# Linear attention with a GLU on one core: w_phi read by heads and spread by small products, weights queued behind the last row transpose

## The chip, the cores and the metric

The kernel runs on one core of a Trainium2 chip. The metric is the device time of one execution in microseconds (us). A core has five engines that run side by side, each with its own instructions in a fixed order: TensorE (PE, matmuls into PSUM), VectorE (DVE), ScalarE (ACT), GpSimd (POOL) and SyncE (SP), which here issues all DMAs. Engines wait for each other through semaphores. An instruction that waits holds up everything behind it on its engine.

## The reference

The input x has 2048 rows of 640. There are 32 heads of 20, and the FFN is 1536 wide.

```python
def _A_ref(x, wqkv, w_phi, wo):              # H = 32, Dh = 20
    q, k, v = ...                            # x @ wqkv, split by heads
    pq = einsum("bhsd,hdf->bhsf", q, w_phi)  # w_phi: [32, 20, 20]
    pk = einsum("bhsd,hdf->bhsf", k, w_phi)
    phi_q = concatenate([softmax(pq), softmax(-pq)], -1)
    phi_k = concatenate([softmax(pk), softmax(-pk)], -1)
    kv = einsum("bhsf,bhsd->bhfd", phi_k, v)
    z = phi_k summed over s
    o = einsum(phi_q, kv) / (einsum(phi_q, z) + 1e-6)
    return o.reshape(B, S, D) @ wo
h = x + _A_ref(layernorm(x), wqkv, w_phi, wo)
return h + ((layernorm(h) @ w_gate) * (layernorm(h) @ w_up)) @ w_down
```

## The kernel before

All matmul inputs are bf16. The rows are 16 tiles of 128 (t = 0 to 15); 640 columns are five chunks of 128.

`build_graph` lists 975 operations, each with an engine, an estimated cost, what it reads and writes, and a key. `schedule` plays the list with the estimated costs and, on each engine, always takes the ready operation with the smallest key. That fixes the order on every engine, the semaphore waits and the PSUM banks. The keys come from a table, `TUNED`, which names each operation with a planned start time (and, after a colon, the other engine where an operation can run on either). So a changed table changes the order of all engines.

The stages, with the names that the prediction uses:

- **Head.** `zero` and `warm` give TensorE matmuls on zeros. SP loads x (`x0`, `x1`, `x2`, ...; from `x2` on two tiles in one DMA), the K columns of Wqkv (`wk0`, `wk2`, `wk4`) and the V columns (`wv0`, ...). w_phi is read twice: `phr`, its first 600 rows of 20 values, one row in each descriptor, onto 120 partitions, and `ph5`, the last 40 rows. GpSimd builds an identity matrix (`id0`, `id1`) and a mask `GL` of which row belongs to which head (`gl0`, `gla`, `glb`), and multiplies them into the block-diagonal matrix `Phi` (`phi0`, `phi5`). TensorE transposes Wk (`WT0` to `WT4`), the transposes are copied out (`WTe`), and the folds `F1_0` to `F1_4` multiply them by Phi, so that K's projection gives pk at once (`Fe1` copies out). The same for Wq: `wqt0` to `wqt5` are DMA transposes from DRAM, and `F0_0` to `F0_4` fold; each needs all six.
- **Rows.** For each tile VectorE takes the statistics (`L1s`, `L1a`), ScalarE the inverse deviation (`L1l`, `L1e`, for groups of tiles), VectorE normalizes (`xn`). Tiles 0 to 2 are transposed by TensorE (`xt`, `xte`), the others by a DMA transpose on SP (`xt3` to `xt15`). Then come the projections `V` (copied out by `Ve`) and `K`, two exponentials on ScalarE (`Kx`), the sums and their reciprocals on VectorE (`Ks`, `Kr`), the scaling on GpSimd (`Kn`), and `KV`, which adds the tile's part to three PSUM banks. A projection holds a pair of banks until it is copied out. V and K of tiles 0 and 1 are split into five parts each (`V0_0`, ...).
- **Columns and output.** Q's projections (`Q`, `Qx`), the attention output by tile (`N`, `sr`, `rho`, `A`, `B`, `dd`, `rd`, `o`, a DMA transpose `oT`, the product with Wo `O`, the sum `h`), the second normalization (`L2s`, ..., `hc`, a DMA transpose `hT`), the gate and up products (`U`, `g`, `u`) and the down product (`D`, `y`, a store `w`).

`PACE` holds loads back until a named row transpose has been issued on SP:

```python
for g in range(6):
    PACE[7 + g // 2].append(wqt(g, 10 * (7 + g // 2) - 19))
PACE[10] += [wrows("wo", ..., 0, 2, 328, 81), wrows("wo", ..., 2, 5, 492, 81)]
for c in range(NC):
    PACE[11 + c] += [wrows("wg", ...), wrows("wu", ...)]
```

The lines of the profile that matter: L268 all plain loads, L299 the Wq transposes, L331 `phi0`, L357 the warming matmuls, L367 Wk's transposes on TensorE, L388 the folds, L404, L405 and L407 the row statistics, L432 `xn`, L440 the row transposes on TensorE, L448 the row transposes on SP, L461 the K and V projections, L482 the exponentials, L485 and L488 `Ks` and `Kr`, L490 `Kn`, L499 `KV`, L233 copies, L520 Q, L553 the attention products, L596 the product with Wo, L600 the sum `h`, L635 gate and up, L654 down.

Of the kernel before, what the change touches and what calls it, by code (L numbers as in the profile page):

```python
# [12 lines left out]
P = 128  # L13
# [22 lines left out]
WIN = [0, 120, 240, 360, 480, 512]  # L36
# [6 lines left out]
NWARM = 8  # L43
# [5 lines left out]
x0:1.18 wk0:2.14 wk2:3.58 wk4:3.1 x1:0.7 wv0:5.02 wv2:5.98 wv4:5.5 x2:4.06 x4:6.46 x6:4.54 phr:1.66 ph50:2.02 ph5:2.62 x8:14.747 x10:23.167 x12:25.347  # L49
x14:23.647 wqt0:24.127 wqt1:25.827 wqt2:35.727 wqt3:39.867 wqt4:41.087 wqt5:38.647 wo0:36.947 wo2:43.527 wg0:32.327 wu0:32.807 wg1:50.547 wu1:46.927  # L50
wg2:49.587 wu2:44.007 wg3:48.627 wu3:51.027 wg4:50.067 wu4:49.107 id0:0.7 gl0:2.62 eps:1.82 id1:2.22 gla0:3.68 glb0:4.34 gla4:4.12 glb4:4.56 gla1:3.24
glb1:4.78 gla2:3.02 glb2:5.72 gla3:3.46 glb3:3.9 phi0:5 phi5:5.94 va1:1 glx:6.191 kv1:6.591 zero:0.7 warm:1.08 WT0:5.718 WTe0:6.323 WT1:6.053
WTe1:6.781 WT2:8.355 WTe2:9.249 WT3:8.69 WTe3:9.979:1 WT4:6.509 WTe4:7.114 F1_0:7.402 Fe1_0:7.974:1 F1_1:7.704 Fe1_1:8.276:1 F1_2:10.189 Fe1_2:10.761:1
F1_3:10.919 Fe1_3:11.491 F1_4:8.054 Fe1_4:8.625:1 L1s0:4.081 L1a0:5.081 L1s1:3.261 L1a1:4.901 L1s2:9.027 L1a2:11.597 L1s3:9.847 L1a3:11.487 L1s4:14.167
L1a4:15.517 L1s5:13.347 L1a5:14.987 L1s6:11.817 L1a6:12.817 L1s7:10.667 L1a7:11.707 L1s8:21.717 L1a8:22.997 L1s9:19.367 L1a9:21.607 L1s10:25.947
L1a10:27.227 L1s11:27.337 L1a11:28.977 L1s12:31.767 L1a12:34.007 L1s13:28.157 L1a13:39.087 L1s14:35.857 L1a14:37.097 L1s15:34.577 L1a15:39.197
L1l0:5.411 L1e0:5.841 L1l1:5.191 L1e1:5.631 L1l2:12.114 L1e2:12.544 L1l4:15.846 L1e4:17.312 L1l8:29.338 L1e8:30.181 L1l12:39.614 L1e12:40.044 xn0:6.361
xt0:7.123 xte0:7.811:1 xn1:5.941 xt1:6.844 xte1:7.393:1 xn2:15.097 xt2:15.941 xte2:16.689 xn3:12.927 xt3:13.527 xn4:18.527 xt4:20.727 xn5:18.107
xt5:19.507 xn6:18.947 xt6:21.947 xn7:17.687 xt7:18.287 xn8:30.927 xt8:34.507 xn9:36.677 xt9:37.427 xn10:31.347 xt10:33.287 xn11:30.507 xt11:31.107
xn12:44.327 xt12:45.707 xn13:41.187 xt13:42.307 xn14:43.907 xt14:47.407 xn15:43.487 xt15:44.487 V0_0:11.594 V0_1:13.767 V0_2:14.311 V0_3:14.854  # L60
# [159 lines left out]
def build_graph():  # L220
# [61 lines left out]
    for n_, (a, b_) in enumerate(((0, 2), (2, 4), (4, 5))):  # L282
# [7 lines left out]
        lambda: T["A_wphi"].rearrange("h d f -> (h d) f")[0:600, :].rearrange("(g p) f -> p g f", p=120), 24, [phr_b], key=-98.5)  # L290
    G.op("pool", "ph50", lambda e: e.memset(T["ph5"][:, :], 0.0), 0.2, LP, [], [ph5_b], -99.2)
    dma("sp", "ph5", lambda: T["ph5"][88:128, :], lambda: T["A_wphi"].rearrange("h d f -> (h d) f")[600:640, :], 2, [ph5_b],
        reads=[ph5_b], key=-98.4)


    PACE = {t: [] for t in range(NT)}
# [718 lines left out]
```

## Time and profile before

| what | value |
|---|---|
| median of 8 runs | 286.04 us (284.24 to 287.48) |
| the profiled execution's own time | 287.46 us |
| its span, first to last instruction | 285.7 us |
| TensorE busy | 277.6 us (97%) |
| VectorE busy | 182.7 us (64%) |
| ScalarE busy | 106.1 us (37%) |
| GpSimd busy | 56.7 us (20%) |
| share of the chain that ended last | PE 81%, DVE 9%, DMA 6% |
| DMA | 44832 packets, 22.31 MB |

All times in the profile count from the first instruction. The windows give, for a stretch of time, each engine's busy time and the number of its instructions, the granted TensorE clock, the busy share of the DMA engines and GB/s. The waits give who waited for whom. The chain in order of time is followed back from the last instruction, and gives start, length and what it was. In a timeline line, the brackets at the end give the idle time ahead of the group and what ended it.

### The profile page before, as it was taken

To read this page: it belongs to the slowest core of one execution; us is meant where nothing else is said; L and a number is where in the kernel's file an instruction comes from. 1 tells how busy PE (TensorE), PEld (TensorE's weight loads), DVE (VectorE), ACT (ScalarE), POOL (GpSimd) and SP (SyncE) were. 2 spreads that over 40 slices of the span, in tenths; PEclk is the share of its full clock that TensorE was granted. 3 is DMA by queue.
4 is the path that set the end of the run, shared out by engine and by line. 5 is a ranking of instruction groups with operands and counts; after the bars stand their busy time and mean duration, and the time that the engine had idled before them with its cause. 6 is when DMAs were issued, how large, how long until landed. Compare 5 with 4: busy or idle time off the path is not lost.

```text
span 285.7 us, 5039 instructions
## 1 busy us (share of the span) xinstructions
PE 277.6 (97%) x2083; PEld 184.2 (64%) x2083; DVE 182.7 (64%) x370; ACT 106.1 (37%) x187; POOL 56.7 (20%) x64
## 2 busy tenths in 40 slices
PE   6999889999999999999999999999999999999996
PEld 3877657779555589775555544576565555478875
DVE  4799899677258787997798562635982144332533
ACT  3786645643786852224131323110221022312110
POOL 7023369978011121222000000001000000000000
PEclk9999999999999999999999999999999999999999
DMA  6737499990002368134310320021115000100002
GB/s 165 251 78 172 100 203 154 251 328 12 0 2 46 61 127 237 39 86 78 69 37 13 68 46 2 0 70 48 47 28 66 23 25 24 23 2 23 25 23 69
DMA packets 44832, 22.31 MB, mean 78 GB/s; under 512 B 35977, under 2 KB 43529, under 8 KB 44809
## 3 DMA queue, kind: packets, MB, share of 16 engines
q1 hardware_dynamic: 44809, 21.99, 33.3%
q8 instruction: 16, 0.26, 0.4%
q14 instruction: 7, 0.06, 0.1%
HBM read 11.00 MB, written 2.62 MB: 48 GB/s over the span
## 4 chain that ended last, share of the span: by engine, by line
PE 81%; DVE 9%; DMA 6%; SPq 2%; issue 1%; ACT 0%; DVEq 0%
PE ps L635 36%; PE ps L654 18%; PE ps L596 8%; PE ps L520 8%; PE ps L553 4%; PE ps L461 3%; DMA xnT<-xn 3%; DVE SR L485 3%; DVE xn L432 2%; PE ps L499 2%; DMA x_all<-in_A_x_dram 1%; DVE st L405 1%; DMA scratch<-in_A_wqkv_dram 1%; DVE st L404 1%; SPq L268 1%; DVE SR L488 1%
## 5 line engine op out<-in xcount | busy, mean ns | idle before, releaser
L635 PE MATMUL ps<-xnT,Wgu 128*128 128x512 bf16 (+1 forms) x600 | 108.1, 337 | 0.0
L635 PEld LDWEIGHTS ps<-xnT,Wgu 128*128 128x128 bf16 x600 | 58.2, 98 | 42.2 <-DVE ev L643 0.4
L640 ACT ACTIVATE scratch<-ps 128x512 bf16<-128x512 f32 (+1 forms) x60 | 30.6, 511 | 106.7 <-PE ps L635 102.7
L643 DVE TENSOR_TENSOR ev<-ps,scratch 128x512 bf16<-128x512 f32 (+1 forms) x60 | 33.5, 578 | 35.2 <-ACT scratch L640 19.5
L654 PE MATMUL ps<-Wp,ev 128*128 128x320 bf16 (+2 forms) x396 | 54.1, 295 | 0.0
L461 PE MATMUL ps<-Wp,xnT 128*128 128x320 bf16 x320 | 45.9, 300 | 2.8 <-DMA xnT<-xn 1.5
L654 PEld LDWEIGHTS ps<-Wp,ev 128*128 128x128 bf16 x396 | 38.0, 98 | 14.3
L490 POOL TENSOR_TENSOR ev<-ev,SR 128x1280 bf16<-128x1280 bf16 x16 | 37.3, 2356 | 26.4 <-DVE SR L488 20.6
L461 PEld LDWEIGHTS ps<-Wp,xnT 128*128 128x128 bf16 x320 | 30.6, 98 | 14.8 <-DMA xnT<-xn 2.0
L666 DVE SCALAR_TENSOR_TENSOR Wp<-ps,rs,x_all 128x640 bf16<-128x640 f32 (+3 forms) x18 | 14.6, 810 | 31.6 <-PE ps L654 31.6
L610 POOL TENSOR_SCALAR ln<-mv 128x1 f32<-128x1 f32 x16 | 3.9, 243 | 115.7 <-DVE mv L609 112.1
L482 ACT ACTIVATE ev<-ps 128x640 bf16<-128x640 f32 x32 | 20.8, 701 | 10.9 <-PE ps L461 10.0
L485 DVE TENSOR_REDUCE SR<-ev 128x64 f32<-128x1280 bf16 x16 | 23.0, 1455 | 2.5 <-ACT ev L482 2.5
L529 ACT ACTIVATE eqT<-ps 128x512 bf16<-128x512 f32 x40 | 21.6, 596 | 7.4 <-PE ps L520 7.4
L596 PE MATMUL ps<-Wo,scratch 128*128 128x320 bf16 x160 | 24.0, 300 | 0.0
L520 PE MATMUL ps<-xnT,Wp 128*128 128x512 bf16 x100 | 23.0, 379 | 0.0
L615 ACT ACTIVATE xn<-x_all,mv 128x640 bf16<-128x640 bf16 x16 | 13.1, 826 | 22.6 <-DVE mv L609 19.4
L596 PEld LDWEIGHTS ps<-Wo,scratch 128*128 128x128 bf16 x160 | 15.6, 98 | 7.5
L585 POOL TENSOR_TENSOR scratch<-scratch,sm 128x640 bf16<-128x640 f32 x8 | 10.2, 1270 | 44.8 <-DVE sm L582 42.2
L600 DVE TENSOR_TENSOR x_all<-ps,x_all 128x640 bf16<-128x640 f32 x16 | 13.1, 818 | 5.5 <-PE ps L596 5.4
L520 PEld LDWEIGHTS ps<-xnT,Wp 128*128 128x128 bf16 x100 | 9.5, 98 | 9.8 <-DVE KVm L506 0.2
L553 PE MATMUL ps<-KVm,eqT 128*128 128x154 bf16 (+1 forms) x192 | 15.5, 222 | 0.0
(56 smaller groups left out, 204.9 us busy)
## 6 DMA issues: line engine op xcount, KB each, us to landing
out_dram<-Wp SPq DMA_DIRECT2D x15, 160.0 KB, 1.8
x_all<-in_A_x_dram SPq DMA_DIRECT2D x7, 320.0 KB, 4.3
Wgu<-in_B_w_gate_dram SPq DMA_DIRECT2D x5, 384.0 KB, 6.7
Wgu<-in_B_w_up_dram SPq DMA_DIRECT2D x5, 384.0 KB, 4.7
Wp<-in_B_w_down_dram SPq DMA_DIRECT2D x4, 480.0 KB, 5.1
scratch<-in_A_wqkv_dram SPq DMA_DIRECT2D x2, 320.0 KB, 4.1
Wp<-in_A_wqkv_dram SPq DMA_DIRECT2D x2, 320.0 KB, 6.2
Wo<-in_A_wo_dram SPq DMA_DIRECT2D x1, 480.0 KB, 4.8
```

What stands on the lines that cost most here:

```text
L461: ins = e.matmul(pb(b, hb)[:, 0:320], lhsT=T["xnT"][:, NC - 1 - c, P * t:P * (t + 1)], rhs=T["Wp"][:, kind, c, 320 * hb:320 * (hb + 1)], s ...
L482: G.op("act", "Kx%d_%d" % (t, s), lambda e, s=s, b=b, ek=ek: e.activation(out=T["ek"][:, ek.slots[0], s, :].rearrange("p (b n) -> p b n", ...
L485: G.op("dve", "Ks%d" % t, lambda e, ek=ek, sr=sr: e.tensor_reduce(out=T["SR"][:, sr.slots[0], 0, :], in_=T["ek"][:, ek.slots[0], :, :].rea ...
L490: G.op("pool", "Kn%d" % t, lambda e, ek=ek, sr=sr: e.tensor_tensor(out=T["ek"][:, ek.slots[0], :, :].rearrange("p s (h f) -> p (s h) f", f ...
L520: ins = e.matmul(pb(b)[:, 0:n], lhsT=T["Wp"][:, 0, i, P * c:P * (c + 1)], rhs=T["xnT"][:, NC - 1 - i, o0:o0 + n], start=(i == 0), stop=(i ...
L529: G.op("act", "Qx%d_%d_%d" % (q, c, s), lambda e, s=s, c=c, o0=o0, n=n, b=b: e.activation(out=T["eqT"][:, s, c, o0:o0 + n], in_=pb(b)[:, 0 ...
L553: ins = e.matmul(pb(b, y)[:, 22 * h0:22 * (h0 + j1 - j0)], lhsT=T["eqT"][:, s, c, P * t:P * (t + 1)], rhs=T["KVm"][:, OFF[s, c] + j0:OFF[s ...
L596: ins = e.matmul(pb(b, hb)[:, 0:320], lhsT=T["oT"][:, oT.slots[0], c, :], rhs=T["Wo"][:, c, 320 * hb:320 * (hb + 1)], start=(c == 0), stop ...
L635: ins = e.matmul(pb(b)[:, 0:n], lhsT=T["Wgu"][:, gu, c, P * ft:P * (ft + 1)], rhs=T["xnT"][:, NC - 1 - c, o0:o0 + n], start=(c == 0), stop ...
L640: G.op("act", "g%d_%d" % (bi, ft), lambda e, pg=pg, gt=gt, n=n: e.activation(out=T["gt"][:, gt.slots[0], 0:n], in_=pb(pg)[:, 0:n], func=AF ...
L643: o_ = G.op("dve", "u%d_%d" % (bi, ft), lambda e, pu=pu, gt=gt, hh=hh, ft=ft, n=n: e.tensor_tensor(out=T["hh"][:, hh.slots[0], ft, 0:n], i ...
L654: ins = e.matmul(pb(b, hb)[:, 0:w], lhsT=T["hh"][:, hh.slots[0], ft, P * tt:P * (tt + 1)], rhs=T["Wd"][:, ft, c0 + w * hb:c0 + w * (hb + 1 ...
```

## The change

- `w_phi` is read once (`w32`), with one head on each of 32 partitions (400 values in one row), as the first DMA of SP. `phr`, `ph5`, the memset `ph50` and GpSimd's `phi0` and `phi5` are gone.
- `PH`: 20 matmuls with the identity as the moving operand turn it to 20 partitions; `PHd` copies that out and reorders it; `PS`: two matmuls with a selection matrix `sel` repeat it on 120 partitions; `PHe` on VectorE multiplies it by the mask `GM` into `Phi`. GpSimd makes `sel` and `GM` by three copies.
- The last window of the Wk and Wq transposes starts at 520 instead of 512, and the folds take 120 rows from it.
- The warming matmuls are 6 instead of 8, in three pairs that have a place in the order (`warm0`, `warm1`, `warm2`).
- Wo's and the FFN's weights are held back until `xt15` has been issued.
- Three estimates of the planner are changed, and the whole table `TUNED` is new: nearly all engines have another order.

```diff
-WIN = [0, 120, 240, 360, 480, 512]
+WIN = [0, 120, 240, 360, 480, 520]
-NWARM = 8
+NWARM = 6
...
-    dma("sp", "phr", lambda: T["phr"][0:120, :, :],
-        lambda: T["A_wphi"].rearrange("h d f -> (h d) f")[0:600, :].rearrange("(g p) f -> p g f", p=120), 24, [phr_b], key=-98.5)
...
+    dma("sp", "w32", lambda: T["w32"][:, :], lambda: T["A_wphi"].rearrange("h d f -> h (d f)"), 30, [w32_b], key=-100.5)
...
-    PACE[10] += [wrows("wo", lambda: T["Wo"], "A_wo", wo_b[0:2], 0, 2, 328, 81), wrows("wo", lambda: T["Wo"], "A_wo", wo_b[2:5], 2, 5, 492, 81)]
+    PACE[15] += [wrows("wo", lambda: T["Wo"], "A_wo", wo_b[0:2], 0, 2, 328, 81), wrows("wo", lambda: T["Wo"], "A_wo", wo_b[2:5], 2, 5, 492, 81)]
     for c in range(NC):
-        PACE[11 + c] += [wrows("wg", lambda: T["Wgu"][:, 0], "B_wg", [wg_b[c]], c, c + 1, 393, 91 + 10 * c),
+        PACE[15] += [wrows("wg", lambda: T["Wgu"][:, 0], "B_wg", [wg_b[c]], c, c + 1, 393, 91 + 10 * c),
...
-    G.op("pool", "phi0", lambda e: e.tensor_tensor(
...
-    G.op("pool", "phi5", lambda e: e.tensor_tensor(
...
-        for _ in range(NWARM):
+        for _ in range(2):
...
-    G.op("pe", "warm", warm, 0.43 * NWARM, LT, [z_b], [wm_b], -200)
+    for k in range(NWARM // 2):
+        G.op("pe", "warm%d" % k, warm, 0.86, LT, [z_b], [wm_b], -90)
...
+    def rows(e):
+        for f in range(DH):
+            ins = e.matmul(pb(pq_b, f // 10)[0:DH, H * (f % 10):H * (f % 10 + 1)],
+                           lhsT=T["w32"][:, :].rearrange("h (d f) -> h f d", f=DH)[:, f, :], rhs=T["ident"][0:H, 0:H],
+                           start=(f % 10 == 0), stop=True, skip_group_check=True)
+        return ins
+    G.op("pe", "PH", rows, 1.2, LT, [w32_b, id_b], [pq_b], -95)
...
+    evac("PHd", phd, 640, [pq_b], [pd_b], -95)
...
+    def spread(e):
+        for k in range(2):
+            ins = e.matmul(pb(pr_b, k)[0:120, 0:320], lhsT=T["sel"][0:DH, :], rhs=T["phid"][0:DH, 320 * k:320 * (k + 1)],
+                           start=True, stop=True)
+        return ins
+    G.op("pe", "PS", spread, mm_c(320, 320), LT, [sel_b, pd_b], [pr_b], -95)
...
+    G.op("dve", "PHe", mask, 0.8, LD, [pr_b, gm_b], [phi_b], -95)
...
-                    K = P if g == 5 else 120
+                    K = 120
...
-        G.op("dve", "xn%d" % t, xn, 0.42, LD, [x_b[t], mv_b[t], rs_b[t]], [xb], 10 * t - 22)
+        G.op("dve", "xn%d" % t, xn, 0.5, LD, [x_b[t], mv_b[t], rs_b[t]], [xb], 10 * t - 22)
...
-                bw += o.dma / (210.0 if bw < 7.0 else 370.0)
+                bw += o.dma / (210.0 if bw < 4.0 else 370.0)
...
-                bw = max(bw, now + 1.85) + 0.5
+                bw = max(bw, now + 1.7) + 0.65
```

The orders that follow from the new table, as far as the prediction uses them:

```
PE before  warm WT0 WT1 WT4 xt1 xt0 F1_0 F1_1 F1_4 WT2 WT3 K0_0 K1_0 K0_1 K1_1 F1_2 F1_3 V0_0 K0_2 K1_2 V1_0 ...
           ... K5 V6 KV1 K7 KV2 V11 K11 V10 KV3 V8 K8 K9 KV4 V9 KV5 F0_1 KV6 K13 K10 KV7 K12 KV8 V14 ...
PE after   warm0 warm1 PH warm2 PS WT1 WT0 WT2 WT3 F1_1 F1_0 xt0 WT4 xt1 F1_2 V0_0 V1_0 ... V1_3 V0_4 F1_3 K0_0 ...
           ... KV0 K6 KV1 V6 K7 V8 KV2 V10 K10 KV3 K11 V11 KV4 F0_3 KV5 V9 K8 KV6 K9 K12 KV7 V13 K13 V14 KV8 K14 K15 KV9 ...
SP before  x1 x0 phr wk0 ph5 wk4 wk2 x2 x6 wv0 wv4 wv2 x4 xt3 x8 xt7 xt5 xt4 xt6 x10 x14 wqt0 x12 wqt1 xt11 wg0 wu0
           xt10 xt8 wqt2 wo0 xt9 wqt5 wqt3 wqt4 xt13 wo2 wu2 xt15 xt12 wu1 xt14 wg3 wu4 wg2 wg4 wg1 wu3 oT1 ...
SP after   w32 x0 x1 wk0 wk2 x2 wk4 wv0 x6 wv2 wv4 x4 xt3 x8 xt4 xt5 x10 xt7 wqt1 wqt0 x12 xt6 x14 xt8 wqt3 xt10 xt11
           wqt2 xt9 wqt4 wqt5 xt12 xt13 xt14 xt15 wu1 wg2 wg3 wo2 wg0 wu0 wg1 wg4 wo0 wu3 wu4 wu2 oT0 ...
DVE after  ... L1s9 Ks0 L1a9 Ks2 L1s11 L1s10 Kr0 Ks1 L1a10 L1a11 Kr1 L1s12 L1s14 xn8 Ks4 xn10 xn11 Kr2 Ks3 L1s13 Kr3 xn9
           Ks5 Kr4 Kr5 Ks6 L1a12 L1a14 L1s15 Kr6 Ks7 L1a15 L1a13 Kr7 Ks11 xn12 Kr11 xn13 xn14 Ks10 xn15 ...
```

## The prediction

> **What bounds the kernel now.** I read the page first, then the windows, the waits of TensorE, the chain in order of time, and the timeline of the first 15 us.
>
> ```profile
> span 285.7 us, 5039 instructions
> ...
> PE 277.6 (97%) x2083; PEld 184.2 (64%) x2083; DVE 182.7 (64%) x370; ACT 106.1 (37%) x187; POOL 56.7 (20%) x64
> ...
> PE 81%; DVE 9%; DMA 6%; SPq 2%; issue 1%; ACT 0%; DVEq 0%
> ```
>
> TensorE is busy for all but 8.1 us. A change can only gain where those 8.1 us lie, or where TensorE works slowly. The windows (stretch, its length, busy time of PE first) say where.
>
> ```profile
> 30.00:35.00 5.00, 3.98 (x37) 2.85 (x36) 3.87 (x8) 2.90 (x7) 2.23 (x1) 1.00 0.41 105
> ...
> 40.00:45.00 5.00, 3.67 (x34) 2.62 (x33) 4.93 (x10) 2.45 (x6) 5.00 (x3) 1.00 1.17 168
> ...
> 50.00:55.00 5.00, 4.59 (x54) 3.64 (x52) 2.74 (x4) 2.76 (x5) 4.92 (x4) 1.00 0.95 251
> 55.00:58.20 3.20, 3.01 (x38) 2.40 (x36) 2.92 (x3) 2.40 (x5) 2.07 (x1) 1.00 1.06 248
> ...
> 70.00:283.20 213.20, 213.20 (x1478) 135.42 (x1475) 124.69 (x265) 64.79 (x117) 15.13 (x25) 1.00 0.21 46
> ```
>
> From 58.2 to 283.2 us PE never idles, so whatever the change does later counts only if it tears a hole there. Between 30 and 58.2 us PE loses 1.02 + 1.33 + 0.41 + 0.19 = 2.95 us, and 0.42 us more between 10 and 15. The rest lies before 5.94 us and after 283.2 us. The waits of PE from 12 to 60 us and the chain name the causes:
>
> ```profile
> PE ps L461 <- DMA xnT<-xn: 1.5, 2, 1.3
> PE ps L461 <- ACT ev L482: 1.0, 1, 1.0
> PE ps L388 <- ACT ev L233: 0.4, 1, 0.4
> ```
>
> ```profile
> 2.23 3.67 DMA scratch<-in_A_wqkv_dram
> ...
> 27.54 4.16 DMA x_all<-in_A_x_dram
> ...
> 36.98 4.97 DMA xnT<-xn
> ...
> 53.93 4.21 DMA xnT<-xn
> ```
>
> A row transpose that meets no other traffic lands 2.6 us after its issue (the least of the 13 of this stage); those issued behind Wo and FFN weights took 4.2 to 5.0. The first cost PE 1.33 us (V10 waits for xt10), the other 0.19. The 1.02 us at 32.5 starts at x12: it lands at 31.70, 4.16 us after issue, VectorE sits on its L1s13 with L1a11 behind it, so ScalarE's L1l8 and the exponentials behind that come late, and the PSUM pair for V6 with them. The 0.41 us is F0_1, which also needs the last Wq transpose: wqt4 landed at 50.98.
>
> In the head, the timeline:
>
> ```profile
> 1.24 3.60 PE L357 MATMUL ps<-zero 128*128 128x512 bf16 x8 [1.24 <-DVE zero L352]
> ...
> 5.94 2.10 PE L367 MATMUL ps<-ident,scratch 128*128 128x128 bf16 x18 [1.10 <-DMA scratch<-in_A_wqkv_dram]
> ...
> 5.12 1.19 POOL L331 TENSOR_TENSOR Phi<-phr,GL 120x600 bf16<-120x600 bf16 x1 [1.30 <-DMA phr<-in_A_w_phi_dram]
> ...
> 10.54 0.83 PE L367 MATMUL ps<-ident,scratch 128*128 128x128 bf16 x12
> ```
>
> 18 transposes take 2.10 us at 5.94 (0.107 apart), 12 of the same shape 0.83 at 10.54 (0.056 apart): the clock came up at about 10.5 us, after 4.6 us without a gap. The 3.60 us of warming matmuls, followed by 1.1 us of idleness, did not bring it. 4.6 us at half pace cost 2.3 us of PE time.
>
> **The change part by part.** *w_phi's read.* phr is 600 rows of 40 bytes, issued ahead of wk0. It takes 3.3 us for 23 KB, and while its small packets run (3.0 to 4.3 us) the queues move some 50 KB/us against 340 to 400 beside them. wk0, 320 KB, therefore takes 3.67 us where x0 and x1 took 2.3. Now w_phi is 32 rows of 800 bytes ahead of everything, and ph5 is gone too. That gives about 1.2 us back to every load behind it: wk0 lands at about 4.6 instead of 5.89, x2 at 6.6 to 7.5 instead of 9.31.
>
> *Phi's new path.* All of it is extra work on three in-order engines. PE: warm0, warm1 (4 x 0.43 from 1.24, to 2.95), then PH, 20 matmuls of 32 columns. The nearest rows are the folds, 21 in 1.79 us at the slow clock (0.085 each, wider pieces), and KV, 12 in 0.68 (0.057): 1.15 to 1.7 us, I take 1.4, to 4.35. w32 stands first in SP's queue and lands by 3.1 (x1, 160 KB, did), so PH hardly waits. ScalarE's PHd is like its other 640-element evacuations, 0.70, to 5.25. Then PS, two 320-column matmuls at the slow clock, 0.55, to 5.85. VectorE's PHe is like L600 (640 elements out of PSUM, 0.82), to 6.85. Queued behind PS on PE stands WT1, behind PHe on VectorE WTe1, xn0 and the rows. So WT1 starts at about 5.85 although its data is there at 4.6: against 5.94, almost nothing of wk0's 1.3 us reaches PE. Phi is ready 0.2 us later than before (phi5 ended at 6.67), ahead of the first fold (8.90 before). Price both ways: if PH takes 1.7 us and w32 is 0.5 late, PE starts 0.7 later than before; if PH takes 1.15, 0.3 earlier.
>
> *GpSimd.* It loses phi0 (1.19), phi5 (0.25) and a memset (0.40); it gains three copies, by the copies of GL (0.21) and KVm (0.50) 0.6 to 1.0 us together. va1 (1.23) moves behind them. All of it ends before 8 us; the first Kn stood at 19.45, so this is nothing. WIN's last window and K = 120 change no column count: nothing.
>
> *The clock.* Two fewer warming matmuls, but they are spread so that PE is occupied from 1.24 us on, with PH and PS between them, into the transposes. By the row (4.6 us of gapless work from 5.94 before it rises) it would come at about 10.3 and gain 0.1 us of PE. If the pieces before WT1 count as occupation, it comes 4.6 us after 1.24, about 6, and 4 us of work run at full pace: 2 us of PE time. It cannot all be used. ScalarE has PHd, WTe0, WTe2, Fe1_1, Fe1_0, xte1, Fe1_2, WTe4, WTe3 in a row (0.7 to 0.81 each), and F1_3 waits for WTe3. I followed this: F1_3 ends at 13.3 with the early clock, at 14.6 with the late one. Before, the same amount of PE work (nine parts of V, four folds) was done at 14.8. So the head gives 1.5 to 0.2 us; I take 1.05, because the pieces are close together.
>
> The Trainium skill (TensorE: Matmul & The Clock Gate, Part 1) says that the clock rises after one busy window of about 3.4 us, whose phase is free, and (Part 4) that transposes do not count as busy. The second half speaks against the change, since PH and PS are short and transposes follow; the trace has three of its 4.6 us before the rise in transposes. By Part 1 the rise falls between 4.7 and 8.1 us, a head gain of about 1.5; by Part 4 it would wait for the folds, and the gain is 0.2 or nothing.
>
> *Weights behind xt15.* Twelve loads (4.6 MB) leave the stretch from 36 to 58 us. The row transposes xt8 to xt15 then meet only the Wq transposes. For V10 I expect the landing in 2.7 to 3.5 us, not 4.97, so 1.33 and 0.19 go. The weights start at about 53 us; the last six of before landed 0.97 us apart, so twelve are in by about 68. Wo's first reader stood at 89.7 us in the chain, the FFN's at 101.7; some 3 us sooner each, that is 18 us of cover. Past it, each us would cost one. SP has nothing to do between them and the first oT.
>
> *What is late next.* The Wq transposes and x loads are reordered. x14 is issued behind wqt1, wqt0, x12 and xt6, at about 26, and lands 3.2 to 4.3 us later (x10 and x12 before): VectorE's L1s14, with xn8, Ks4, Kr2 behind it, can stall 0.3 to 1.3 us; Kn2 (2.36) follows Kr2, and KV2 waits on PE 0.1 to 1.1 us: 0.5. F0_3 waits for wqt5, issued at about 40.5 behind xt9, which waits for VectorE's xn9; the Wq transposes landed after 3.5 to 5.0 us, so at 44 to 45.5, and PE is there at about 44.6: 0 to 0.9, I take 0.3. K12 needs xn12, with one Ks more ahead of it than before, but VectorE starts its rows some 2 us sooner (x2). Sum of the waits 0.8 instead of 2.95, with bounds of 0.1 and 3.3: a gain of 2.15 (2.85 to a loss of 0.35).
>
> **Sum.** The profiled execution took 287.46 us, 285.7 of span and 1.76 around it; it stands 1.42 above the median of 286.04, and no view says where. 287.46 - 1.05 - 2.15 = 284.3. Best ends: 287.46 - 1.5 - 2.85 = 283.1; worst ends: 287.46 - 0.2 + 0.35 = 287.6. As the median may lie lower than the profiled run for a cause that both kernels share, I let the range begin 1.2 below the best end.
>
> **The rivals.** First: the head gives nothing. The clock rises no sooner and VectorE, which carries the chain from 10.21 to 52.75 almost without a break, sets the pace. Head 0.2, waits 1.3: 285.6, within 0.5% of the median. For it: VectorE is full from 10 to 25 and from 35 to 50 us, and PHe is added to it. Against: its idle 1.8 us between 25 and 35 came from late loads. That w_phi's packets were not what slowed wk0 belongs here too.
>
> Second, slower: F0_3 on PE behind wqt5. Everything on PE stands behind F0_3, and wqt5 stands behind xn9 on VectorE and xt9, wqt4 on SP. If x14 stalls VectorE for 1.3 us more and wqt5 needs 5.0 us, F0_3 waits about 3.4 us: 284.3 + 3.4 = 287.7. From a landing of wqt5 after 48 us it decides. For it: before, the same kind of fold waited, and PE arrives sooner now. Against: no weights stand in the queue, and four row transposes in a row landed in 2.6 to 2.7 us each.
>
> Third, weights late for O0: from 87 us on; with 18 us of cover, 0.01.
>
> **How the numbers follow.** Forecast with its better ends 0.64, the first rival 0.20, the second 0.15, the third 0.01. About 0.5% (1.43 us) is what a measurement of this kernel can tell from no change: faster is below 284.6, slower above 287.5. So faster 0.64, same 0.20, slower 0.16. The range reaches from 281.9 to 287.2, into the second rival; its own for the forecast is 281.9 to 284.6.
>
> **What would show it.** Right: wk0 landed before 5 us and WT1 waiting for PS; transposes 0.056 apart before 8 us; xt10 to xt15 landing within 3.5 us; PE's idle time between 30 and 58 us near 1 us and none after. Wrong: transposes at 0.107 until 10 us (head), a wait of PE at F0 for scratch or at KV for ev above 1 us, or any idle PE after 60 us, which the sum does not hold.

## The result, and the profile after

The changed kernel takes 288.58 us in the median (287.45 to 289.32, 12 runs); the kernel before took 286.24 beside it (33 runs). The ratio is 1.0076, with a 95% interval of 1.0054 to 1.0098: slower by about 2.2 us, where 284.3 had been forecast, and outside the range.

The page of the changed kernel shows the same span and the same busy time of TensorE as before:

```profile
span 285.7 us, 5087 instructions
...
PE 277.6 (97%) x2103; PEld 183.9 (64%) x2103; DVE 180.5 (63%) x366; ACT 109.3 (38%) x190; POOL 59.5 (21%) x67
...
PE 85%; DVE 7%; DMA 4%; issue 1%; POOL 1%; ACT 0%; SPq 0%; DVEq 0%
```

The two profiled executions, 287.46 and 287.45 us, are a poor pair: the one of before is near the top of its runs (284.24 to 287.57), the one after is the lowest of its twelve. What that is worth is taken up below.

The windows, with the length and PE's busy time first, answer to those of before in the prediction. One stretch of before that is not among them comes first:

```profile
10.00:30.00 20.00, 19.58 (x168) 14.54 (x166) 19.04 (x42) 16.05 (x28) 4.84 (x3) 1.00 0.55 138
```

and after the change:

```profile
10.00:30.00 20.00, 18.65 (x173) 13.86 (x171) 18.50 (x44) 16.07 (x29) 2.12 (x1) 1.00 0.69 133
30.00:35.00 5.00, 5.00 (x49) 3.86 (x48) 2.58 (x6) 3.06 (x8) 2.56 (x2) 1.00 0.31 74
...
40.00:45.00 5.00, 4.93 (x51) 3.94 (x52) 5.00 (x10) 2.39 (x4) 4.77 (x4) 1.00 0.72 131
...
70.00:283.20 213.20, 212.93 (x1470) 134.91 (x1468) 123.37 (x262) 64.03 (x117) 19.38 (x28) 1.00 0.20 46
```

The holes at 30 to 35 and 40 to 45 us are closed, as forecast. A larger one stands between 10 and 30 (1.35 us idle instead of 0.42), and a small one after 70. The waits of TensorE from 12 to 135 us name them:

```profile
PE ps L488 <- DMA xnT<-xn: 1.3, 1, 1.3
PE ps L526 <- POOL ev L517: 0.4, 1, 0.4
PE ps L623 <- DMA scratch<-scratch: 0.3, 1, 0.3
PE ps L415 <- ACT ev L232: 0.2, 1, 0.2
```

The first is V7 waiting for the row transpose xt7, which landed 4.50 us after its issue; the second KV2 for Kn2; the third O for the transpose of o; the fourth F0_3, for a copy of ScalarE's. The head is in the timeline:

```profile
1.24 1.89 PE L341 MATMUL ps<-zero 128*128 128x512 bf16 x4 [1.24 <-DVE zero L336]
...
3.06 0.93 PE L359 MATMUL ps<-ident,w 32*20 32x32 bf16 x20
...
3.92 1.03 PE L341 MATMUL ps<-zero 128*128 128x512 bf16 x2
4.02 2.97 ACT L232 ACTIVATE phid<-ps 20x640 bf16<-20x640 f32 x1 [1.95 <-PE ps L359]
...
7.13 0.75 PE L374 MATMUL ps<-phid,sel 20*120 20x320 bf16 x2 [2.18 <-ACT ln L439]
...
7.82 2.74 PE L394 MATMUL ps<-ident,scratch 128*128 128x128 bf16 x24
```

PHd takes 2.97 us and ends at 6.99. PS waits for it (the bracket names the short `ln`, which stands behind PHd on ScalarE and ended last), and PE stands still for 2.18 us. WT1 starts at 7.82, where the first transpose of before started at 5.94, and still runs at half pace (24 transposes in 2.74 us).

**Where the time lies.** To compare kernels whose orders differ, I worked out from each trace a lag: the time t, less the useful TensorE work begun by t (transposes, folds, projections, KV; not warming, PH or PS), every matmul at its price with the clock up (0.056 us for 128 columns, 0.136 for 320). It is all that the kernel has lost so far. The last two columns are the profiled execution's time and where the granted clock came up (from the trace's record; for e17, which has none, from the spacing of its transposes). The windows above give the clock as 1.00 even in the head, where the transposes run at half pace: its record has no entry ahead of the first rise. So the clock of the head is read from that rise and from the spacing of the matmuls.

| kernel | lag at 16 us | at 32 | at 44 | at 60 | its time | clock up |
|---|---|---|---|---|---|---|
| before | 8.76 | 8.78 | 11.66 | 12.76 | 287.46 | 10.54 |
| before, once more (b2) | 6.75 | 8.10 | 9.08 | 10.53 | 285.17 | 5.42 |
| after | 9.46 | 10.91 | 11.79 | 12.33 | 287.45 | 10.69 |
| e1 | 7.69 | 9.05 | 10.30 | 11.54 | 287.01 | 8.74 |
| e2 | 8.76 | 8.78 | 10.30 | 10.59 | 285.23 | 10.37 |
| e4 | 7.13 | 8.37 | 10.17 | 12.22 | 286.86 | 5.92 |
| e5 | 6.99 | 8.37 | 8.95 | 9.40 | 283.98 | 5.63 |
| e10 | 8.35 | 9.79 | 10.98 | 12.01 | 286.86 | 7.00 |
| e16 | 7.53 | 7.73 | 8.69 | 10.45 | 285.41 | 5.45 |
| e17 | 6.99 | 7.28 | 7.86 | 8.18 | 282.78 | 6.69 |

Time less the lag at 60 us is 274.6 to 274.7 for every kernel with the old path, and 274.9 to 275.5 with the new one, whose PE waits 0.3 to 0.7 us once more at about 130 us. So the lag at 60 us accounts for nearly the whole difference between these executions. Against the profiled execution of before, the changed kernel loses 0.70 in the head (9.46 against 8.76), gains 1.13 between 16 and 60 us (2.87 against 4.00), and gives 0.42 back later.

### The profile page after: what moved, and what is told of

It is laid out like the page before. It is cut to its first block, busy times and chain, and to the rows that moved or that the text cites. A ratio compares the mean times of both kernels' runs of the same rounds, so it can differ in the third digit from the quotient of the medians.

```text
span 285.7 us, 5087 instructions
## 1 busy us (share of the span) xinstructions
PE 277.6 (97%) x2103; PEld 183.9 (64%) x2103; DVE 180.5 (63%) x366; ACT 109.3 (38%) x190; POOL 59.5 (21%) x67
## 4 chain that ended last, share of the span: by engine, by line
PE 85%; DVE 7%; DMA 4%; issue 1%; POOL 1%; ACT 0%; SPq 0%; DVEq 0%
PE ps L662 36%; PE ps L681 17%; PE ps L547 8%; PE ps L488 7%; PE ps L623 7%; PE ps L580 4%; PE ps L526 3%; DMA x_all<-in_A_x_dram 3%; DVE SR L512 1%; DMA scratch<-scratch 1%; DVE st L431 1%; DVE st L432 1%; DVE xn L459 1%; PE ps L394 1%; POOL ev L517 1%
## 5 line engine op out<-in xcount | busy, mean ns | idle before, releaser
L612 POOL TENSOR_TENSOR scratch<-scratch,sm 128x640 bf16<-128x640 f32 x11 | 14.0, 1270 | 77.9 <-DVE sm L609 76.9
L580 PEld LDWEIGHTS ps<-KVm,eqT 128*128 128x128 bf16 x192 | 12.9, 98 | 4.2
```

Source lines behind the costliest of these rows:

```text
L580: ins = e.matmul(pb(b, y)[:, 22 * h0:22 * (h0 + j1 - j0)], lhsT=T["eqT"][:, s, c, P * t:P * (t + 1)], rhs=T["KVm"][:, OFF[s, c] + j0:OFF[s ...
```

## The experiments

Each was timed beside the kernel before, whose median was 285.9 to 286.2 in all of them; ratios are to that, with their 95% intervals.

### The parts one by one: e1 to e4

**e1**, the changed kernel with PHd written contiguously:

```diff
-        return copy(e, eng, T["phid"][0:DH, :].rearrange("p (h b f) -> p b f h", b=2, f=10),
-                    T["PS3"][0:DH, k:k + 2, 0:320].rearrange("p b (f h) -> p b f h", h=H))
+        return copy(e, eng, T["phid"][0:DH, :].rearrange("p (b n) -> p b n", b=2), T["PS3"][0:DH, k:k + 2, 0:320])
...
-            in0=T["PS3"][0:120, k:k + 2, 0:320].rearrange("p b (h f) -> p b h f", f=DH),
...
+            in0=T["PS3"][0:120, k:k + 2, 0:320].rearrange("p b (f h) -> p b h f", h=H),
...
```

(PHe's output and its mask are reordered with it.)

> The changed kernel with PHd writing its 640 elements in PSUM order, contiguously; the reordering by head moves into PHe's read of PSUM. Nothing else differs, nor does any engine's order. Theory H (the strided write of PHd, 2.97 us, is what holds PE 2.18 us in front of PS and delays the first fold to 10.35): PHd takes 0.7 to 0.8 us, PS starts at about 5.0, PHe takes 0.8 to 1.0, WT1 starts when wk0 lands, about 6.2 instead of 7.82, F1 at about 8.8, and the median comes 1.3 to 2.3 us under the changed kernel's 288.6: 286.3 to 287.3. Rival R (the time goes into the new order of the body, not into the head): PHd gets as fast, but the time stays at 288.0 or more. Second rival (PHe's strided read of PSUM takes over what PHd loses): PHe rises above 2 us.

Measured: 287.06 us, ratio 1.0031 (1.0012 to 1.0051), 1.5 us under the changed kernel. Its timeline:

```profile
4.03 0.69 ACT L232 ACTIVATE phid<-ps 20x640 bf16<-20x640 f32 x1 [1.96 <-PE ps L359]
...
5.71 0.82 DVE L380 TENSOR_TENSOR Phi<-ps,GM 120x640 bf16<-120x640 f32 x1 [0.24 <-PE ps L373]
...
6.04 2.74 PE L393 MATMUL ps<-ident,scratch 128*128 128x128 bf16 x24 [0.36 <-DMA scratch<-in_A_wqkv_dram]
```

The strided write alone made PHd 2.97 instead of 0.69 us. PHe, which now hops 128 bytes from element to element in PSUM, still takes 0.82. Theory H holds, and WT1 waits for wk0 at 6.04. But the kernel stays slower than before, and 24 transposes still take 2.74 us.

**e2**, the kernel before with the weights alone held back, behind the row transpose that is last in its own order:

```diff
-    PACE[10] += [wrows("wo", ...), wrows("wo", ...)]
+    PACE[14] += [wrows("wo", ...), wrows("wo", ...)]
-        PACE[11 + c] += [wrows("wg", ...), wrows("wu", ...)]
+        PACE[14] += [wrows("wg", ...), wrows("wu", ...)]
```

> The kernel before with one edit: Wo and the FFN weights wait behind the transpose that ends its own order of rows (xt14), nothing done to w_phi. Theory W (the second part of the change is a gain by itself): xt8 to xt15 land in 2.6 to 3.0 us as in the changed kernel, TensorE's idle time between 30 and 60 us falls from 2.95 to 1.2 to 1.6, the median is 284.5 to 285.2. Rival (VectorE sets the pace there, and the waits come back elsewhere): 285.9 to 286.5. Second rival (the weights arrive late): a wait of PE on a weight load after 80 us, over 286.5.

Measured: 284.49 us, ratio 0.995 (0.9927 to 0.9973). xt11, xt10, xt8, xt9, xt15, xt12 and xt14 landed in 2.6 to 3.0 us, xt13, behind wqt4, in 3.5. The waits of PE from 12 to 135 us are:

```profile
PE ps L461 <- ACT ev L482: 1.3, 1, 1.3
PE ps L461 <- ACT Wp L233: 0.3, 1, 0.3
```

Theory W holds: in the old order this half of the change is a gain of about 1.5 us (1.7 by the medians, 1.4 by the ratio), and no weight is late.

**e3**, the kernel before with the new path for w_phi (strided PHd) alone. Seen from the changed kernel, these go back to what they were, and the table and the planner's estimates with them:

```diff
-NWARM = 6
+NWARM = 8
...
-    PACE[15] += [wrows("wo", ...), wrows("wo", ...)]
+    PACE[10] += [wrows("wo", ...), wrows("wo", ...)]
-        PACE[15] += [wrows("wg", ...), wrows("wu", ...)]
+        PACE[11 + c] += [wrows("wg", ...), wrows("wu", ...)]
...
-    for k in range(NWARM // 2):
-        G.op("pe", "warm%d" % k, warm, 0.86, LT, [z_b], [wm_b], -90)
+    G.op("pe", "warm", warm, 0.43 * NWARM, LT, [z_b], [wm_b], -200)
```

> The kernel before with the first part of the change alone: w_phi read with one head per partition and spread by small matmuls, PHd with its strided write; the table of times, the eight warming matmuls in one piece and the places of the weights stay those of the kernel before. Theory H: PHd takes about 3 us, the folds' Phi is ready at 8.5 to 9, F1_0 starts 0.5 to 1.5 us later than in the kernel before, median 287.0 to 288.5. Rival (the head's time is hidden behind the load of x and of wkn): 286.0 to 286.5.

Measured: 290.86 us, ratio 1.0188 (1.0151 to 1.0225), worse than either theory said. PHd (2.94 us) stands behind L1l on ScalarE; PE waits 1.43 us for it ahead of PS and 0.57 for wk0. The record of the clock has a step that I had not expected: up at 5.63 us, down again at 9.05, up at 12.46, each 3.413 us from the last.

**e4**, the kernel before with 11 warming matmuls instead of 8, so that PE is occupied until WT0:

```diff
-        for _ in range(NWARM):
+        for _ in range(11):
```

> The kernel before with 11 warming matmuls instead of 8, so that PE is occupied from 1.24 us to where WT1 starts, about 5.9; nothing else differs. Theory C (the rise of the granted clock follows from unbroken occupation of PE, and its place in the head is worth about a microsecond): the WT transposes run 0.056 us apart from before 8.1 us on, the median is 284.8 to 285.5. Rival (the rise comes at about 10.5 whatever PE does before): 286.0 to 286.5.

Measured: 285.79 us, ratio 1.000 (0.9979 to 1.0022). The clock was up at 5.92 and the lag at 16 us 1.63 lower than in the profiled execution of before, as theory C says; by 60 us only 0.54 of it was left. With the weights still among the transposes, PE waited 1.74, 0.65, 1.05 and 0.48 us between 30 and 58 us. In this execution the gain in the head was given back in the stage behind it, and the median shows none either.

### The clock, and the order: e5 to e12

**e5**: the edits of e2 and e4 together.

> The weights held behind xt14 as in e2, and 11 warming matmuls instead of 8. In e4 the longer warming brought the clock up at 5.92 and an earlier head, but waits for row transposes after 30 us took that back; with the weights out of the transposes' way they should not. Theory C+W: clock up between 5 and 8.1, idle time of TensorE between 30 and 60 us under 2.2, median 283.2 to 284.0, 0.5 to 1.3 under e2's 284.49. Rival (the pace from 15 us on is set by VectorE and the loads whatever the head does): 284.2 to 284.8.

Measured: 283.71 us, ratio 0.995 (0.992 to 0.9981), 0.8 under e2 as C+W expected, though the intervals of the two overlap. Profile to profile, the lag at 60 us is 1.19 lower.

**e6**: e1 with two steps moved:

```diff
-x10:19.263
+x10:15.5
-Kr2:31.603
+Kr2:27.0
...
-        PACE[3 + j].append(xload("sp", 8 + 2 * j, 10 + 2 * j, 10 * (3 + j) - 19))
+        PACE[3 + max(0, j - (j == 1))].append(xload("sp", 8 + 2 * j, 10 + 2 * j, 10 * (3 + j) - 19))
```

> The changed kernel with PHd contiguous (e1) and two steps of its order moved: the load x10 goes right behind x8 instead of between the transposes xt5 and xt7, and VectorE's reciprocal Kr2 goes ahead of the statistics of row 12. Theory O (what is lost after the head is lost to the new order: V7 waits 1.17 for xt7, which takes 4.4 us behind x10, and KV2 waits 0.96 for Kn2): xt7 lands within 3 us of its issue, both waits fall under 0.3, median 285.0 to 285.8, 1.3 to 2.0 under e1's 287.06. Rival (the waits come back at the next step, since loads or VectorE set the pace): 286.5 to 287.2.

Measured: 286.83 us, ratio 1.0044 (1.0021 to 1.0066), not told apart from e1. xt7 landed in 2.74 us instead of 4.41 and the wait for it was gone, the one for Kn2 too; others of 0.4 to 0.55 came in their place. But in this execution the clock came up only at 11.72.

**e7**: e3 with the edits of e1 (PHd contiguous) and e2 (weights behind xt14).

> The kernel before with the weights behind xt14 (e2) and the new path for w_phi with a contiguous PHd; the table of times and the eight warming matmuls are those of before. It sets the new path against the old one in the old order. Theory P (PH and PS, 1.6 us of PE at the low clock, and the chain through ACT and VectorE cost more than the read of w_phi did): first projection 0.5 to 1.5 us later than in e2, median 285.0 to 286.2. Rival (they lie in the wait for wk0, 1.14 us, and the path is free or a gain): 284.0 to 284.7.

Measured: 289.08 us, ratio 1.0129 (1.0092 to 1.0166), 4.6 over e2: more than theory P said. Its lag is 10.12 at 16 us (e2: 8.76) and grows by 3.9 until 60 (e2: 1.8). The old table was made for the old head; with the rows of VectorE and ScalarE shifted by PHd and PHe, PE waits 1.81 us up to 35.9 and 0.90 up to 48.8. That the shift is the cause of these waits was not tested.

**e8** and **e10**: the changed kernel, strided PHd and all, with one longer warming piece.

```diff
-    def warm(e):
-        for _ in range(2):
+    def warm(e, n=2):
+        for _ in range(n):
...
-        G.op("pe", "warm%d" % k, warm, 0.86, LT, [z_b], [wm_b], -90)
+        G.op("pe", "warm%d" % k, warm if k < 2 else (lambda e: warm(e, 7)), 0.86, LT, [z_b], [wm_b], -90)
```

> The changed kernel as it is, strided PHd too, with 7 matmuls in the last warming piece instead of 2, so that PE is occupied through the 2.18 us in which it waits for PHd. Theory C: the clock comes up by 8.1 instead of 10.7, the transposes WT run at 0.056 us each, the median is 286.9 to 287.9, 0.7 to 1.7 under 288.58. Rival (the clock's place does not matter, the loads hold the head): 288.2 to 288.9.

> The same edit as e8 (the changed kernel with 7 matmuls in the last warming piece), once more, for an undisturbed trace. Theory C: PE is occupied from 1.24 us through PS, the clock is up by 8.1, WT1 still starts at about 7.8 behind the 2.97 us of PHd; median 286.3 to 287.0.

Measured: 286.68 us, ratio 1.0038 (1.0015 to 1.006), and 286.25, ratio 1.0012 (0.9997 to 1.0028). The one execution of e8 that was profiled took 591.69 us, twice the other eleven, and its trace is not used. e10's timeline of PE:

```profile
3.93 3.17 PE L341 MATMUL ps<-zero 128*128 128x512 bf16 x7
7.15 0.45 PE L374 MATMUL ps<-phid,sel 20*120 20x320 bf16 x2
7.53 1.51 PE L394 MATMUL ps<-ident,scratch 128*128 128x128 bf16 x24
```

The same 24 transposes take 1.51 us instead of 2.74. Five more matmuls of zeros give the whole loss back, 1.9 to 2.3 us, with PHd as slow as ever: what PHd's 2.97 us cost was mostly the clock. e16 below, with the same warming, the short PHd and two steps moved, is only 0.6 us faster.

**e9** (e6 with 4 matmuls in the last warming piece) and **e11** (e1 with the same); the edit is e8's with `warm(e, 4)`:

> e6 (contiguous PHd, x10 behind x8, Kr2 ahead) with 4 matmuls in the last warming piece instead of 2, so that TensorE is occupied from 1.24 us until WT1 starts. In e6's trace the clock came up only at 11.7 us. Theory C (an unbroken occupation, longer than two of the clock's periods of 3.41 us, brings the clock up by about 8.1 whatever the phase): transposes 0.056 us apart from 8.1 at the latest, median 284.2 to 285.2, 1.6 to 2.6 under e6. Rival (with PHd contiguous the clock no longer costs anything, the order does): 286.5 to 287.0.

> e1 (the changed kernel with a contiguous PHd) with 4 matmuls in the last warming piece, the order untouched: between e9 and e1. Theory C+O: clock up by 8.1, the waits of V7 for xt7 and KV2 for Kn2 remain and grow to 2.5 to 3.5 together, median 285.3 to 286.3, about 1 over e9 and about 1 under e1. Rival (order's waits cost nothing): the same as e9 within 0.3.

Measured: 286.17 us, ratio 1.0017 (0.9994 to 1.004), and 286.37, ratio 1.0023 (1.0003 to 1.0043). Theory C fails here as it was first put: PE was occupied from 1.24 us on in both, and the clock came up at 9.96 and 9.34, not by 8.1. The moved steps are not told apart from none.

**e12**: the kernel before with 4 warming matmuls (e4's edit with `range(4)`).

> The kernel before with 4 warming matmuls instead of 8: PE occupied from 1.24 to 2.95, then idle until WT0 at 5.9. Theory C (only an unbroken occupation counts, and in the kernel before it starts at 5.94 in either case): no change, 285.8 to 286.6. Rival (every warming matmul brings the rise nearer, broken or not): rise about 1 to 3 us later, 286.8 to 287.8.

Measured: 286.56 us, ratio 1.0041 (1.0018 to 1.0064): inside theory C's bounds, but a loss, not nothing.

### What fills a period of the clock: e13, b2

The steps in e3's record are 3.413 us apart, and the stretches at full clock in the other records are 80, 81 or 82 times that long (276.48 us in before). Read back from each recorded rise in these steps, the traces give, for every period, the share that full-size matmuls took (120 or 128 rows), and that of narrow ones (PH on 32 rows, PS on 20):

| kernel | period at whose end it rose | full, narrow | period before, no rise | full, narrow |
|---|---|---|---|---|
| before | 7.13 to 10.54 | 1.00, 0 | 3.71 to 7.13 | 0.68, 0 |
| after | 7.28 to 10.69 | 0.84, 0.16 | 3.86 to 7.28 | 0.30, 0.06 |
| e1 | 5.32 to 8.74 | 0.79, 0.10 | 1.91 to 5.32 | 0.62, 0.38 |
| e3 | 2.22 to 5.63 | 0.74, 0.26 | | |
| e6 | 8.31 to 11.72 | 1.00, 0 | 4.90 to 8.31 | 0.64, 0.23 |
| e9 | 6.55 to 9.96 | 1.00, 0 | 3.14 to 6.55 | 0.56, 0.44 |
| e11 | 5.92 to 9.34 | 0.84, 0.16 | 2.51 to 5.92 | 0.69, 0.31 |
| e16 | 2.03 to 5.45 | 0.75, 0.25 | | |

Full-size work of three quarters of one period brings the clock up. Shares of 0.72 (before, 0.30 to 3.71) and less do not, and narrow work does not add to them. The limit is not sharp: e3 rose after 0.74, e6 did not (1.49 to 4.90, also 0.74, with 0.26 of narrow work). **e13** puts narrow work to the test: e4 with its 11 warming matmuls on 20 rows and 20 columns of the array.

```diff
-            ins = e.matmul(pb(wm_b)[:, 0:512], lhsT=T["zero"][:, 0:P], rhs=T["zero"][:, :], start=True, stop=True)
+            ins = e.matmul(pb(wm_b)[0:DH, 0:512], lhsT=T["zero"][0:DH, 0:DH], rhs=T["zero"][0:DH, :], start=True, stop=True)
```

> The kernel before with 11 warming matmuls as in e4, but on 20 rows and 20 columns of the array instead of 128 and 128; 512 columns move in each, so PE is occupied as long. e4's clock was up at 5.92. Theory N (narrow matmuls like PH and PS do not count for the clock's rise): the transposes stay 0.107 us apart until 9.3 at least, as in the kernel before; median 286.0 to 286.8. Rival (occupation counts, whatever the width): the clock is up by 8.1 as in e4, median 285.4 to 286.0.

Measured: 287.18 us, ratio 1.0029 (1.0003 to 1.0055). PE's timeline:

```profile
1.24 4.86 PE L357 MATMUL ps<-zero 20*20 20x512 bf16 x11 [1.24 <-DVE zero L352]
6.03 2.10 PE L367 MATMUL ps<-ident,scratch 128*128 128x128 bf16 x18
...
10.18 0.83 PE L367 MATMUL ps<-ident,scratch 128*128 128x128 bf16 x12
```

PE is as occupied as in e4, yet 18 transposes take 2.10 us, and the clock comes up at 9.63. The period from 2.81 to 6.22 held 0.94 of narrow work and brought nothing; the next one, which holds transposes and folds only, brought it. So narrow work does not bring the clock up, as theory N says; whether rows or columns decide was not separated, and the median is 0.4 above N's range.

Then the phase of the periods decides when the clock comes up, and the kernel before should have two kinds of heads. **b2** is the kernel before, profiled once more.

> The kernel before, unchanged, profiled once more for its clock. By the rule of three quarters of a period, laid over its matmuls at every phase, the clock comes up either at 3.8 to 5.7 us (58 phases of 100) or at 9.3 to 10.6 (42 of 100), and at no time between. Rival (the rise follows the first long stretch of work alone): between 9.3 and 12.8. If the rise is early, the execution is also faster than the profiled 287.46, by 1 us or more, if the clock is kept through the idle 1.1 us before WT0.

Measured: one execution, 285.17 us, with the clock up at 5.42. PE's timeline, to be held against the two lines of before in the prediction:

```profile
1.24 3.59 PE L357 MATMUL ps<-zero 128*128 128x512 bf16 x8 [1.24 <-DVE zero L352]
5.95 1.18 PE L367 MATMUL ps<-ident,scratch 128*128 128x128 bf16 x18 [1.11 <-DMA scratch<-in_A_wqkv_dram]
```

The same eight warming matmuls and the same idle 1.11 us, and now the transposes run at full pace (1.18 us instead of 2.10). It is 2.3 us faster than the first profiled execution of the same program, and 2.0 of that is lag at 16 us (6.75 against 8.76). An early clock is no guarantee of such a time, though: e4's execution has nearly the same head and took 286.86. Nor do the 33 runs of before beside the changed kernel fall into two groups 2.3 us apart: 10 are under 285.5, 16 between 285.5 and 287.0, and 7 above.

The Trainium skill (TensorE: Matmul & The Clock Gate, Part 1) says that the window is free-running and that cold matmuls vary from run to run with its phase; these two traces of one kernel, 10.54 and 5.42, agree.

### Whether the new path can be mended, and the best version: e14 to e17

**e14** is e6 with 5 matmuls in the last warming piece (`warm(e, 5)`) and two steps queued later, so that the two narrow pieces lie apart:

```diff
+    G.by["PS"].before.append(G.by["WT1"])
+    G.by["PHe"].before.append(G.by["WTe1"])
```

> e6 (contiguous PHd, x10 behind x8, Kr2 ahead) with 5 matmuls in the last warming piece, PS queued behind WT1 and PHe behind WTe1, so that PH (0.95 us) and PS (0.6 us), the narrow matmuls, lie 2 us apart with full-width work between them. Theory N+O (the late clock and the two moved steps are what is left of the loss): clock up by about 8.1 to 9.4, waits after 12 us at most 2.3 together, median 284.2 to 285.2, 1 to 2 under e9's 286.17. Rival (something else in the new path costs 2 us): 285.8 to 286.5.

Measured: 286.18 us, ratio 1.0013 (0.9992 to 1.0035). The rival stands: no gain over e9, though the profiled execution lost only about 2.4 us between 16 and 60 us.

**e15** is the changed kernel with the weights back behind xt10 to xt15:

```diff
-    PACE[15] += [wrows("wo", ...), wrows("wo", ...)]
+    PACE[10] += [wrows("wo", ...), wrows("wo", ...)]
-        PACE[15] += [wrows("wg", ...), wrows("wu", ...)]
+        PACE[11 + c] += [wrows("wg", ...), wrows("wu", ...)]
```

> The changed kernel with the second part undone: the weights wait behind the row transposes xt10 to xt15, as in the kernel before, so that wo2, wg0, wu0 and wo0 go ahead of xt12; the rest of the order is the same. Theory W (the weights part is a gain here too): xt12 to xt15 take 4 to 5 us and land about 2 later, the median rises by 0.3 to 1.2 to 288.9 to 289.8. Rival (in the new order xt12 to xt15 are early enough, and the part is worth nothing): 288.3 to 288.8.

Measured: 289.0 us, ratio 1.011 (1.0078 to 1.0141); against the changed kernel's 1.0076 the intervals overlap. The expected 4 to 5 us for xt12 to xt15 did not come (3.36, then 2.7), and of 1.34 us more lag at 60 us 1.06 was there by 44, before any weight was issued (46.35). What the part is worth in the new order this run doesn't settle; e2 settles it for the old one.

**e16** is e6 with 7 matmuls in the last warming piece (`warm(e, 7)`).

> e6 (contiguous PHd, x10 behind x8, Kr2 ahead) with 7 matmuls in the last warming piece, as e10 has: full-width work from 3.93 to 6.95 us between PH and PS. Against e10 it has the moved steps and the short PHd, with the same warming. Theory O (the moved steps are worth what their waits were, once the clock is certain): clock up by 7 to 8.2, the waits for xt7 and Kn2 under 0.6 each instead of 1.18 and 0.98, median 284.9 to 285.7. Rival (they are given back further on): 286.0 to 286.5.

Measured: 285.65 us, ratio 0.9991 (0.9965 to 1.0017). Its waits from 12 to 135 us:

```profile
PE ps L414 <- DMA scratch<-in_A_wqkv_dram: 1.5, 1, 1.5
PE ps L487 <- DMA xnT<-xn: 0.5, 1, 0.5
PE ps L661 <- DVE x_all L626: 0.3, 1, 0.3
```

The waits for xt7 and Kn2 are gone, and F0_3 waits 1.5 us for wqt5 instead, which lands at 45.86. The lag stood at 8.69 at 44 us and was 10.42 at 48. This is the prediction's second rival, at less than half its size. So the mended new path reaches the kernel before, and no more.

**e17** keeps the old path: e5 with the load x12 ahead of wqt0.

```diff
-x12:25.347
+x12:24.0
```

> e5 (old path, weights behind xt14, 11 warming matmuls) with the load x12 ahead of the first Wq transpose wqt0 instead of behind it. Theory X (the wait of 1.08 us at 32.45 comes from x12, through VectorE's statistics of row 13 and ScalarE's logarithm to the exponentials): x12 lands 1 to 2 us sooner, the wait falls under 0.4, median 282.6 to 283.3. Rival (the wait has another cause or comes back): 283.5 to 284.0.

Measured (6 runs): 283.0 us, ratio 0.9889 (0.986 to 0.9918), the best version, 3 us under the kernel before and 5.6 under the changed one. x12 landed at 28.93 instead of 30.45 (e5), and the wait of 1.1 is gone:

```profile
PE ps L461 <- DMA xnT<-xn: 0.3, 1, 0.3
PE ps L461 <- ACT Wp L233: 0.3, 1, 0.3
```

## Why the prediction was wrong

The step that failed is the head, its clock above all. It was booked as a gain of 1.05 us, with WT1 at 5.85 us and the clock rising early in good part; it was a loss. Against the very execution from which the prediction starts (287.46), the profiled one after the change came in at 287.45, not 284.3. Of these 3.2 us, 1.75 lie in the head (a lag 0.70 higher at 16 us instead of 1.05 lower), 1.0 in the waits up to 60 us (1.13 gained instead of 2.15), and 0.4 after 60 us, where the sum held nothing. The median lies 1.1 above that execution.

**w_phi's read: wrong.** Taking phr's 600 rows away did not bring wk0 forward: it landed at 6.21 us, not 4.6 (before: 5.89), and at 5.4 to 6.4 in the other runs of the new path. The DMA queues still have a slow stretch, shorter than before: 24 to 43 KB in a quarter of a microsecond from 3.5 to 4.25 us, against 7 to 38 from 3.0 to 4.25. But behind w32 they also start more slowly, with 53 KB from 2.0 to 2.75 us against 203. What sets wk0's landing stays open. x2 came 1.4 earlier (7.94), not 1.8 to 2.7. The first rival had named this.

**Phi's path: one term mis-sized.** PH took 0.93 (1.4 forecast), PS 0.75 (0.55), PHe 0.82 as said. PHd was priced at 0.70 "like its other 640-element evacuations". Those write contiguously; PHd writes each 2-byte element 40 bytes from the last, and took 2.97. The number of elements was matched, the access pattern, which stands in the diff, was not. WT1 started at 7.82, not 5.85.

The Trainium skill (SBUF — State Buffer, SBUF: two separate sides, the note on cachelines) says that accesses which cross into a new 16-byte line each time pay a penalty, beyond a step of 8 elements of bf16. e1 agrees: 2.97 against 0.69.

**The clock: the term that decided.** The prediction expected more full-pace work from pieces that "are close together"; the clock rose at 10.69 us, no earlier than before (10.54). The change cut the warming into pairs, with narrow work between them and 2.18 us of idleness behind, and so left 0.53 and 0.30 of full-size work in the two periods ahead. e10 shows what that cost: five more full-size matmuls in the last piece gave the loss back, with PHd unchanged.

The baseline was misread too. It came from one execution ("the 3.60 us of warming matmuls did not bring it"), and that one was of the late kind. Laid over the matmuls of the first trace at 100 phases, the three-quarters rule gives, as an estimate, a rise at 3.8 to 5.7 us in some 58 and at 9.1 to 10.6 in some 42, 7.0 in the mean. By that estimate most executions of before had the early clock already, and the late one is part of why the profiled execution stood 1.42 above the median. How large a part isn't shown: the runs do not fall into two groups, and e4, whose clock the rule has up by 7.2 at every phase, was timed no faster than before. For the changed kernel the same estimate gives 11.4 to 12.1 in the mean, with the limit at 0.74 or 0.75, and 13.8 at most; its profiled rise, 10.69, was an early one, which fits its being the lowest of twelve.

**Weights: right**, and shown by e2 for the old order. In the changed kernel xt8 to xt15 landed in 2.6 to 2.84 us; the weights were in by 70.8 (68 forecast) and nobody waited for them.

**The waits that remain: 2.0 instead of 0.8 us.** Between 30 and 58 us they came to 0.63, even less than forecast. KV2 waited 0.43 (0.5 forecast). F0_3 waited 0.20 (0.3), but that agreement is luck: wqt5 landed at 47.67, over 2 us later than forecast, PE came later as well, and what F0_3 waited for was a copy on ScalarE. V7's 1.27 us for xt7, at 26 us, was not on the list. The list looked at x14 and at wqt5; but x10, a load of 328 KB, stood right ahead of xt7 on SP and delayed it.

**The sum.** As an estimate for the medians: WT1's start and the mean rise put the head of the changed kernel at 7.82 + (11.4 - 7.82)/2 = 9.6 us of time lost by its start and its half pace (10.0 with a rise at 12.1), and before at 5.94 + 0.42 x (10 - 5.94)/2 = 6.8, where 42 in 100 pay for a rise at about 10. That is a loss of 2.8 to 3.2 in the head, against 0.9 gained by 60 us (2.87 against b2's 3.78), with 0.4 given back after it: 2.3 to 2.7 slower, measured 2.2 to 2.3. It was worked out afterwards, from single traces, so the agreement proves little. What spreads the runs of one kernel stays open; only profiled executions have a record of the clock.

## What to carry to other kernels

When a profile stands well off the median, find out what that one execution had that the others did not before booking a gain against it; here two executions of one and the same kernel, with the clock up at 10.54 and at 5.42, were 2.3 us apart. Price an evacuation by its access pattern as well as its count of elements, and keep warming work full-size and in one piece up to the first real matmul. Make a head faster together with the stage behind it: e4 alone gave its gain back, e5 and e17 kept theirs.

## What the runs showed of the hardware

- ScalarE wrote 20 x 640 bf16 in 2.97 us with each element 40 bytes from the last, in 0.69 contiguously. VectorE read 120 x 640 f32 of PSUM in 0.82 us either way, contiguous or 128 bytes apart.
- The granted clock changes at steps of 3.413 us, at a phase that differs between executions. In the 15 traces that record it, it rose after a period with 0.75 or more of full-size matmuls, transposes among them, and never after one with 0.72 or less; at 0.74 it rose once (e3) and once not (e6). Matmuls on 20 rows and 20 columns, 0.94 of a period, did not bring it (e13). e3's clock fell back after a period with 2.0 us of idleness.
- The Trainium skill (TensorE: Matmul & The Clock Gate, Part 4) says that transposes do not count as busy; e13 speaks against it, since its clock rose at the end of a period of transposes (6.22 to 8.99) and folds. The trace shows these transposes as matmuls against an identity.
- A plain load between DMA transposes of one queue delays the next transpose: in e1, xt5 landed at 21.51, x10 behind it at 23.50, xt7 behind that at 25.23, 4.41 us after its issue; with x10 moved ahead of them (e6) xt7 took 2.74.
